# One attention-plus-MLP kernel: batch 0 mixed in transposed form in PSUM with its mask added by TensorE, and Q/K of batches 2 to 7 loaded twice as token pairs

## Chip, cores and metric

The kernel runs on one core of one Trainium2 chip. The metric is the device time of one execution in microseconds (us), the median of several runs. Here the time of a run is 1.8 us above the span (first to last instruction) that its profile shows. Each run is marked fast or slow in the record, because some executions of a kernel come out slower than the rest. The profile of before is of one further run (356.0 us), whose state the record calls unknown.

Engines: PE is TensorE (matmuls), PEld its weight loads, DVE VectorE, ACT ScalarE, POOL GpSimd, SP the queue that stores the output. "The queue" below is the one whose DMAs POOL issues; all loads of inputs that are cast from fp32 to bf16 go through it. PSUM is the memory into which the matmuls write. The granted clock is the share of PE's full clock that the profile shows as granted to it.

## The reference

Sliding-window attention (window 64, causal) on 8 batches of 8 heads, 576 tokens, head size 64, followed by a token-mixing low-rank step and an MLP:

```python
scores = (q @ k.T) / 8;  mask: 0 <= pos_q - pos_k < 64;  x = softmax(scores) @ v      # per head
h = x.T @ U @ V          # U (576, 32), V (32, 576): mixes tokens
u = x + h.T
out = u + relu(u @ w_ch1) @ w_ch2                                                     # (512, 2048), (2048, 512)
```

Inputs and output are fp32; the kernel computes matmuls in bf16.

## The kernel before

The 4608 tokens are cut into nine chunks of 512. The MLP of a chunk is 16 `ch1` pieces (four matmuls into `psA`, a ReLU on ACT or DVE) and 16 `ch2` pieces (four matmuls into `psU`). Attention of batch b + 1 is woven into the MLP of chunk b: every step of it is put behind a numbered piece, its slot. Batch 0 has no MLP to hide in; it is the prologue.

```python
RUN = [18, 18, 6, 2, 1, 2, 1, 6]        # consecutive tokens in one run of a K/Q load, by batch
PAIRED = [True] * 5 + [False] * 3       # True: 32-bit transpose, score matmuls of 32 rows, twice as many
                                        # False: loaded twice, 16-bit transpose, score matmuls of 64 rows
# ... (cut)
def KT(x, n):                           # transpose of raw K or Q on DVE
    ...
    nc.vector.transpose(                # the form for PAIRED False
        out=dst[:, n * S : (n + 1) * S].rearrange("q (m p e) -> q m e p", p=32, e=r), ...)
def SC(n):                              # scores of a tile on PE, exp on ACT, mask by multiplying on DVE
def PV(t):                              # 16 matmuls with V, 1/sum and product on DVE -> x
def UM(ts):  ...                        # hh = U.T x;  VM: un = x + V.T hh;  UT: transpose un on PE, copy to uT
# ... (cut)
load_v(0, both=True)                    # V of batch 0 comes twice, the second time shifted by 64 tokens (vB)
# ... (cut)
DVE_RELU = (1, 3, 5, 7, 9, 11, 13)      # ch1 pieces whose ReLU is on DVE; the others are on ACT
PLACE = {"VC": [0], "S": [1, 1, 4, 4, 7, 7], "PV": [10, 10, 13, 13, 15],
         "KT": [8, 9, 11, 12, 14, 16, 18, 19],              # KT of the batch after
         "U": [17], "V": [19, 20, 21], "UT": [21, 22, 23, 24, 25]}
PLACE_1 = {"KT": [6, 7, 8, 9], "S": [10, 10, 13, 13, 16, 16], "VC": [18],
           "PV": [20, 20, 22, 22, 24], "U": [26], "V": [28, 29, 30], "UT": [29, 30, 31, 31, 32]}
turn_over(24)                           # matmuls on zeros that keep PE busy; more between the steps of batch 0
```

`VC` copies V into its shifted form `vB` for the later batches (`pair_v`).

The softmax here doesn't subtract the row's maximum and nothing guards it: scores larger than these inputs give would overflow.

## Time and profile before

| | before |
|---|---|
| median time of three runs | 354.2 us (353.8 to 354.7) |
| PE busy | 327.1 us, 92% of the span of 354.1 |
| first `psA` matmul (end of prologue) | 32.2 |
| chunk 0 | 41.0 us |
| chunks 1, 2, 3, 4 | 35.6, 35.7, 35.5, 35.5 us |
| chunk 5 | 45.3 us |
| chunk 6, then 7 (no attention) | 34.1, 27.6 us |

A chunk's length is the time from its first `psA` matmul to the next chunk's first, read from the timeline of PE. This one table tells more than the shares of busy time: PE is the bound in every chunk, so a chunk is long where PE waits or its clock is low.

From the page of before: the span in 40 slices of 8.85 us, busy tenths, the granted PE clock in tenths of full speed, and the busy share of the DMA engines.

```profile
span 354.1 us, 7252 instructions
...
PE   8868997989999999999999999947899999999995
...
PEclk9958998999999999999999999999899999999999
DMA  7999999999999699959991911000010011011011
```

Counted from 1, the dips of PE are slices 1 to 4 (prologue), 7 and 9 (chunk 0) and 27 to 29 (chunk 5); in slices 3, 4, 7 and 29 the clock is down with it. The DMA row is full for the first 13 slices, 115 us.

The prologue, as a table of stretches (start:end, its length, busy time of PE, PEld, DVE, ACT and POOL with the number of instructions, granted clock, DMA share, GB/s):

```profile
8.60:15.60 7.00, 6.96 (x176) 3.68 (x176) 5.71 (x10) 4.45 (x6) 3.76 (x5) 1.00 2.90 155
15.60:25.20 9.60, 5.58 (x87) 3.17 (x87) 4.50 (x11) 1.43 (x4) 7.29 (x11) 0.63 3.07 135
25.20:32.20 7.00, 5.51 (x32) 2.23 (x32) 3.18 (x6) 2.93 (x5) 1.81 (x3) 0.77 1.16 212
```

From 15.6 to 25.2 PE works 5.6 of 9.6 us at a clock of 0.63: PV waits for the second copy of V. Two of PE's waits there, from the timeline (in brackets the idle time before, and what ended it; for a third, of 1.5 us to 19.0, the profile names nothing that ended it):

```profile
17.27 0.22 PE L322 MATMUL xr<-vB,pts 128*64 128x65 bf16 x1 [0.90 <-DMA vB<-in_v_dram]
...
22.92 0.23 PE L322 MATMUL xr<-vB,pts 128*64 128x65 bf16 x1 [1.29 <-DMA vB<-in_v_dram]
```

Chunk 5, from the chain of waits (start, us, what):

```profile
225.98 2.10 DVE kt L241
...
228.60 2.00 DVE qt L241
...
232.79 2.00 DVE kt L241
234.80 1.91 DVE qt L241
...
238.82 2.09 DVE kt L241
241.57 2.09 DVE qt L241
...
246.11 1.97 DVE qt L241
```

Batch 7's transposes, with runs of 6 tokens, take about 2 us each on DVE, and they are the chain: the ReLUs and PV products of chunk 5 stand behind them. With runs of 2, batch 5's transposes of the same form took 0.76 to 0.82 us.

### The profile page before, as it was taken

What the parts mean: (1) busy time and instruction counts of PE and PEld (TensorE: products, weight loads), DVE (VectorE), ACT (ScalarE), POOL (GpSimd) and SP (SyncE); (2) the same over time, 40 slices, a digit from 0 to 9 for tenths busy, and PEclk for the clock granted to TensorE, in tenths of its full rate; (3) what the DMA queues carried; (4) which work ended last, traced back from release to release, by engine and by line L of the source; (5) the groups of instructions that cost most, each with busy time, mean ns of one, the idle gap of its engine ahead of it and who ended that gap; (6) DMA issues with size and microseconds to landing.
All of it is one profiled execution on the core that took longest, in us unless ns stands there. A gap on an engine that the chain in (4) does not pass through costs nothing.

```text
span 354.1 us, 7252 instructions
## 1 busy us (share of the span) xinstructions
PE 327.1 (92%) x3046; PEld 155.6 (44%) x3046; DVE 207.1 (58%) x343; ACT 110.9 (31%) x177; POOL 137.3 (39%) x213
## 2 busy tenths in 40 slices
PE   8868997989999999999999999947899999999995
PEld 3433443445454445544444444422445454444442
DVE  5743846679654864578558855899456543313311
ACT  1604450155224523352235233510225232401300
POOL 8572328899999379927961300000000000000000
PEclk9958998999999999999999999999899999999999
DMA  7999999999999699959991911000010011011011
GB/s 127 141 154 212 206 165 135 175 146 128 111 178 172 61 83 168 171 37 97 174 181 11 58 61 61 2 0 31 30 61 2 0 61 59 0 61 59 0 48 74
DMA packets 101553, 32.78 MB, mean 93 GB/s; under 512 B 87568, under 2 KB 95248, under 8 KB 101520
## 3 DMA queue, kind: packets, MB, share of 16 engines
q0 software_dynamic: 94928, 22.43, 77.7%
q1 hardware_dynamic: 6592, 9.88, 8.1%
q8 instruction: 24, 0.39, 0.5%
q14 instruction: 9, 0.07, 0.1%
HBM read 45.27 MB, written 9.44 MB: 154 GB/s over the span
## 4 chain that ended last, share of the span: by engine, by line
PE 63%; DVE 14%; DMA 13%; issue 4%; POOL 3%; ACT 1%; DVEq 0%; POOLq 0%
PE psU L458 33%; PE psA L436 22%; DMA vA<-in_v_dram 8%; DMA w1b<-in_moe_w_ch_dram 3%; DVE qt L241 3%; DVE kt L241 2%; DVE c L445 2%; PE sc L288 2%; PE tpu L406 2%; DVE xs L332 2%; PE psv L371 2%; PE xr L322 2%; DMA qr<-in_q_dram 1%; DVE un L387 1%; ACT pts L296 1%
## 5 line engine op out<-in xcount | busy, mean ns | idle before, releaser
L458 PE MATMUL psU<-w2b,c 128*128 128x512 bf16 x576 | 137.3, 384 | 0.0
L436 PE MATMUL psA<-uTc,w1b 128*128 128x512 bf16 x576 | 131.3, 380 | 1.1 <-ACT uTc L411 0.7
L447 ACT ACTIVATE c<-psA 128x512 bf16<-128x512 f32 x81 | 48.5, 598 | 112.0 <-PE psA L436 112.0
L458 PEld LDWEIGHTS <-c 128*128 128x128 bf16 x576 | 54.3, 99 | 62.7 <-issue 6.5
L436 PEld LDWEIGHTS <-w1b 128*128 128x128 bf16 x576 | 53.8, 98 | 63.1 <-issue 1.3
L467 DVE TENSOR_TENSOR osb<-psU,un 128x512 f32<-128x512 f32 x36 | 25.0, 694 | 80.2 <-PE psU L458 80.2
L445 DVE TENSOR_SCALAR c<-psA 128x512 bf16<-128x512 f32 x63 | 42.9, 686 | 21.5 <-PE psA L436 21.3
L125 POOL DMA_DIRECT2D kr<-in_k_dram x76 | 47.6, 627 | 11.1 <-DMA w2b<-in_moe_w_ch_dram 4.2
L125 POOL DMA_DIRECT2D qr<-in_q_dram x76 | 47.0, 619 | 8.8 <-DVE pts L303 4.5
L131 POOL DMA_DIRECT2D vA<-in_v_dram x32 | 28.4, 894 | 37.5 <-PE xr L322 24.7
L296 ACT ACTIVATE pts<-sc 128x768 bf16<-128x768 f32 x48 | 36.6, 809 | 17.3 <-PE sc L288 15.7
L303 DVE TENSOR_TENSOR pts<-pts,mask 128x768 bf16<-128x768 bf16 x48 | 26.4, 556 | 18.9 <-ACT pts L296 15.7
L411 ACT COPY uTc<-tpu 128x512 bf16<-128x512 bf16 x32 | 18.8, 586 | 46.8 <-PE tpu L406 46.8
L322 PE MATMUL xr<-vB,pts 128*64 128x65 bf16 x320 | 16.9, 202 | 12.5 <-DVE xs L332 5.8
L332 DVE TENSOR_TENSOR xs<-xr,rcp 128x512 bf16<-128x512 f32 (+1 forms) x40 | 27.6, 691 | 1.4
L387 DVE TENSOR_TENSOR un<-psv,xs 128x512 bf16<-128x512 f32 (+1 forms) x38 | 24.3, 685 | 5.9 <-PE psv L371 5.7
L322 PEld LDWEIGHTS <-pts 128*64 128x64 bf16 x576 | 13.6, 115 | 25.9 <-DVE xs L332 14.3
L288 PEld LDWEIGHTS <-kt 32*64 32x64 bf16 (+1 forms) x1040 | 14.3, 105 | 11.8 <-issue 11.8
L288 PE MATMUL sc<-qt,kt 32*64 32x128 bf16 (+5 forms) x1040 | 17.5, 215 | 0.4 <-DVE qt L235 0.4
L406 PEld LDWEIGHTS <-un 128*128 128x128 bf16 x144 | 11.2, 100 | 13.0 <-issue 6.5
L508 PE MATMUL unread<-idle 128*128 128x512 bf16 (+1 forms) x52 | 15.3, 427 | 1.3 <-DVE idle L155 1.3
L371 PE MATMUL psv<-hh,vrep 128*128 128x512 bf16 x40 | 13.2, 392 | 3.5 <-DVE un L387 3.0
(51 smaller groups left out, 143.1 us busy)
## 6 DMA issues: line engine op xcount, KB each, us to landing
out_dram<-osb SPq DMA_DIRECT2D x36, 256.0 KB, 2.3
kr<-in_k_dram POOLq DMA_DIRECT2D x72, 72.0 KB, 4.1
qr<-in_q_dram POOLq DMA_DIRECT2D x72, 72.0 KB, 3.9
vA<-in_v_dram POOLq DMA_DIRECT2D x32, 128.0 KB, 4.7
w2b<-in_moe_w_ch_dram POOLq DMA_DIRECT2D x2, 1024.0 KB, 21.4
kr<-in_k_dram POOLq DMA_DIRECT2D x4, 288.0 KB, 9.4
qr<-in_q_dram POOLq DMA_DIRECT2D x4, 288.0 KB, 10.2
vB<-in_v_dram POOLq DMA_DIRECT2D x16, 64.0 KB, 6.8
```

Source lines behind the costliest of these rows:

```text
L125: nc.gpsimd.dma_start(out=o, in_=i)
L131: nc.gpsimd.dma_start(out=va[:, t, :, 0:D], in_=v[b, :, t * P : (t + 1) * P, :].rearrange("h p d -> p h d"),)
L288: nc.tensor.matmul(sc[half * W : (half + 1) * W, g, (a - lo) * W : (z - lo) * W], operand("k", g, jj, e, kb * W, (kb + 1) * W), operand("q ...
L296: nc.scalar.activation(out=dst, in_=sc[:, :, 0 : PB * W].rearrange("p g (n w) -> p g n w", w=W), func=ACT.Exp, scale=scale,)
L303: nc.vector.tensor_tensor(out=dst, in0=dst, in1=mask[:, m0 : m0 + PB, :].unsqueeze(1).to_broadcast([P, 2, PB, W]), op=ALU.mult,)
L322: nc.tensor.matmul(xr[r0 : r0 + W, h // 4, (h % 4) * VW : (h % 4 + 1) * VW], pts[:, g, jj * NB + blk, :], rhs, start=True, stop=True,)
L332: nc.vector.tensor_tensor(out=x[lo:hi, t, :, :].rearrange("p (a h) d -> p a h d", a=2), in0=xv[:, :, :, 0:D], in1=rcp[lo:hi].to_broadcast( ...
L387: nc.vector.tensor_tensor(out=u_tiles[g][rs, :], in0=ps[rs, n, :], in1=xt[n][rs], op=ALU.add)
L436: nc.tensor.matmul(ps[:], w1b[:, dc, i * P : (i + 1) * P], uTc[:, dc, :], start=(dc == 0), stop=(dc == NDC - 1),)
L445: nc.vector.tensor_relu(out=c1[i][:], in_=ps[:])
L447: nc.scalar.activation(out=c1[i][:], in_=ps[:], func=ACT.Relu)
L458: nc.tensor.matmul(acc[t][:], c1[i][:, t * P : (t + 1) * P], w2b[:, i, :], start=(i == 0), stop=(i == NFC - 1),)
```

## The change

Two main things at once, and the ReLU split, the places and the load order that go with them.

1. Q and K of batches 2 to 7 are all loaded twice with runs of two tokens (`PAIRED` False), with 8 larger DMAs per batch instead of 16 or 32. That removes the slow transposes of chunk 5 and gives batches 2 to 4 the 64-row score matmuls, at twice the bytes for those three batches.
2. Batch 0: V is loaded once; the mask is added as a bias of -1e30 by an identity matmul; u of batch 0 is mixed in transposed form. x is transposed into four banks of PSUM, the four `UP` matmuls add the mixing term there, and four copies give uT. That takes the place of V, UT and their serial copies.
3. ReLUs on DVE go from seven to five per chunk. Batches 1, 2 and 3 get later places, the first half of `w2` is now loaded before batch 1's K/Q, and the K/Q loads of batches 3 and 4 are issued from later slots (23 and 13, before 10 and 4). Batch 0's V is shifted into `vB` by copies, for two of its tiles on DVE and for two on POOL.

The core of the diff (long; cut at "..."):

```diff
-    RUN = [18, 18, 6, 2, 1, 2, 1, 6]
-    PAIRED = [True] * 5 + [False] * 3
+    RUN = [RP, RP] + [2] * (B - 2)
+    PAIRED = [True, True] + [False] * (B - 2)
...
+        def SC0(n):                       # batch 0: bias by TensorE, no mask multiply
...
+                    nc.tensor.matmul(sc[:, g, 0 : PB * W], ident[:], bias[...], start=True, stop=False)
...
+        def XT(t):                        # x transposed into PSUM
+            def f():
+                for dc in range(NDC):
+                    nc.tensor.matmul(xT0[:, dc, t * P : (t + 1) * P], x[:, t, 2 * dc : 2 * dc + 2, :]..., ident[:],
+                                     start=(t == 0), stop=False)
...
+        def UP():
+            for dc in range(NDC):
+                nc.tensor.matmul(xT0[:, dc, :], hh["sb"][:, dc * P : (dc + 1) * P], vrep[:, W : W + CH],
+                                 start=False, stop=True)
+            for dc in range(NDC):
+                copy = dve_copy if dc % 2 else nc.scalar.copy
+                copy(out=uT_of(0)[:, dc, :], in_=xT0[:, dc, :])
...
-    DVE_RELU = (1, 3, 5, 7, 9, 11, 13)
+    DVE_RELU = (1, 4, 7, 10, 13)
...
     PLACE_1 = {
-        "KT": [6, 7, 8, 9],
-        "S": [10, 10, 13, 13, 16, 16],
-        "VC": [18],
-        "PV": [20, 20, 22, 22, 24],
-        "U": [26],
-        "V": [28, 29, 30],
-        "UT": [29, 30, 31, 31, 32],
+        "KT": [16, 17, 19, 20],
+        "S": [19, 19, 21, 21, 23, 23],
+        "VC": [24],
+        "PV": [25, 25, 27, 27, 28],
+        "U": [29],
+        "V": [30, 31, 31],
+        "UT": [31, 31, 32, 32, 32],
     }
...
+    KT_3 = [17, 18, 20, 22, 24, 26, 28, 30]          # batch 3's transposes, in chunk 1
...
+    xT0 = psum["x0"].tile([P, NDC, CH], FP32, name="xT0")
...
-    turn_over(24)
+    turn_over(26)
...
-        turn_over(6 if n == 1 else 2)
+        turn_over(8 if n == 1 else 2)
...
+    load_w2(0, 8)
+    load_kq(1)
+    load_w2(8, 16)
+    load_v(1)
```

## The prediction

> **What bounds it now.** TensorE: the page gives PE 92% busy, and the chain of waits is 63% PE. An MLP chunk without attention takes 27.6 us (first psA to first psA, 294.96 to 322.59 in the chain); nine make 249 us. A chunk with a batch's attention takes at best 34.1 us (260.8 to 295.0, no wait of PE), usually 35.5. Three stretches are worse (chain, timeline):
> - 0 to 32.2 us, prologue. Scores end at 15.1; then PV waits for the second copy of V (vB DMAs; PV tiles start at 15.6, 17.3, 20.4, 22.9, 24.1), with a granted clock of 0.63 (windows, 15.6:25.2). U, V and UT run serially from 25.2.
> - Chunk 0, 32.2 to 73.3, 41.1 us: PV of batch 1 waits 3.1 us for vB, whose input lands only near 54; clock 0.84 in 52:62.5; a serial UT tail.
> - Chunk 5, 215.6 to 260.8, 45.3 us. Eight transposes of batch 7 with runs of 6 take 2.0 to 2.2 us each on DVE, against 0.73 to 0.82 with runs of 2 (batch 5, same form). PE waits there 3.4 + 2.7 + 1.0 us and more behind DVE, and the clock falls to 0.91.
>
> **What changes.**
> 1. Runs of 2 for batches 2 to 7. Chunk 5: 8 x 1.3 = 10 us less DVE, so it becomes an ordinary chunk: -10 us. Batches 2 to 4 go from 208 32-row score matmuls (1.94 us, chain) to 104 64-row ones (1.38): -0.55 us each. They pay 8 transposes (6.2 us) for 4 (3.0), but two ReLUs per chunk leave DVE (-1.4 us). Net -0.3 us per chunk.
> 2. Prologue: V loads once (0.6 MB, about 5 us of queue at the 135 GB/s seen); vB copies are about 0.2 us on DVE (64x2080 took 0.69). The mask multiply (0.56 us) leaves DVE for two bias matmuls per tile, about 0.35 us of PE. U, V, UT (7 us) become hh, four matmuls and four PSUM copies (about 3.5 us). PV should end near 20, first psA at 24 to 25: -7.5 us. Batch 0's adds move into chunk 0: +1.3 us of PE there.
> 3. Chunk 0: 27.6 + batch 1 (about 9 us PE) + 1.3 + a later-placed, serial UT tail (3 us) and small waits: about 42.5, no shorter than before. So the prologue's gain survives to about 67 us, minus 1.
>
> DMA: batches 2 to 4 load 2.36 MB instead of 1.18. POOL issues fall from 16 or 32 per batch at 0.6 us to 8 at about 0.95 (1024-descriptor V issues cost 0.88). Batch 6 moved twice as many packets in 21 us of issuing, so I estimate 13 to 17 us per batch, within a 35 us chunk.
>
> **Sum.** 67 + 35.3 + 4 x 35.1 + 34.1 + 27.6 + 27.6 + 4 = 336. Nearly all of it is on PE's path: about -10 chunk 5, -6.5 prologue and chunk 0, -1.5 elsewhere.
>
> The Trainium skill, "TensorE: Matmul & The Clock Gate", Part 1, says idle windows of about 3.4 us halve the clock; the 0.63 and 0.84 above agree. Fewer waits should give about 1.0 from 16 us on.
>
> **Right or wrong shows in**: first psA at 24 to 26; second chunk's at 66 to 69; no transpose above 0.9 us after batch 1; chunk 5 near 35; score bursts of 0.46.
>
> **What would spoil it**: the queue, now carrying twice the bytes for batches 2 to 4, lands K/Q of batch 3 or 4 after its transpose's place, so DVE stalls in order and PE with it (up to 8 us); POOL's copies of V delay the weight issues; a cold clock in the prologue; the bunched end of chunk 0.
>
> Chances: faster 0.95, within 2% 0.04, slower 0.01. Range 331 to 343.

## The result, and the profile after

The median went from 354.4 us (before, run again in these rounds) to 342.6 us. The ratio is 0.966, with an interval of 0.960 to 0.972: 3.4% faster. (A ratio here is the mean time of one kernel's fast runs over the mean of the other's in the same rounds, so not quite the ratio of the two medians.) The time lies in the predicted range, but the forecast gain was 18 us and the measured one 12.

The chunks of all versions, from the timeline of PE (us; the second column is where the prologue ends, the fourth is where chunk 1 starts; prologue and chunk 0 together):

| version | first psA | chunk 0 | chunk 1 starts | 1 | 2 | 3 | 4 | 5 | median |
|---|---|---|---|---|---|---|---|---|---|
| before | 32.2 | 41.0 | 73.2 | 35.6 | 35.7 | 35.5 | 35.5 | 45.3 | 354.4 |
| my prediction | 24.5 | 42.5 | 67 | 35.3 | 35.1 | 35.1 | 35.1 | 35.1 | 336 |
| after | 28.5 | 46.2 | 74.7 | 35.7 | 35.0 | 34.2 | 35.0 | 34.2 | 342.6 |
| pairs_alone | 31.6 | 42.7 | 74.3 | 41.8 | 35.6 | 34.8 | 35.6 | 34.8 | 350.6 |
| pairs_late | 33.0 | 41.2 | 74.2 | 34.3 | 35.6 | 34.8 | 35.6 | 34.8 | 344.2 |
| batch0_alone | 28.3 | 45.1 | 73.4 | 36.4 | 35.1 | 34.9 | 34.9 | 44.6 | 352.0 |
| relu_7 | 27.6 | 45.9 | 73.5 | 35.2 | 35.6 | 34.8 | 35.6 | 34.8 | 344.7 |
| four_tiles | 26.4 | 43.7 | 70.0 | 35.7 | 35.0 | 34.2 | 35.0 | 34.2 | 339.1 |
| few_fillers | 27.2 | 45.7 | 72.9 | 35.4 | 35.0 | 34.2 | 35.0 | 34.2 | 341.6 |
| chunk0_early | 27.8 | 39.9 | 67.7 | 34.3 | 35.0 | 34.2 | 35.0 | 34.2 | 336.3 |
| early_four | 26.7 | 44.0 | 70.7 | 34.2 | 35.0 | 34.2 | 35.0 | 34.2 | 338.8 |
| all_three | 25.4 | 45.9 | 71.3 | 34.3 | 35.0 | 34.2 | 35.0 | 34.2 | 339.0 |
| v1_first | 27.1 | 38.6 | 65.7 | 40.2 | 35.0 | 34.2 | 35.0 | 34.2 | 339.3 |
| v1_first_few | 23.9 | 40.9 | 64.8 | 39.0 | 35.0 | 34.2 | 35.0 | 34.2 | 337.7 |
| kt3_later | 26.9 | 38.6 | 65.6 | 33.9 | 35.0 | 34.2 | 35.0 | 34.2 | 332.3 |

The row of after says it: chunks 1 to 5 together give 13 us (11 of them chunk 5), and the prologue with chunk 0 gives nothing. It ends 1.5 us later than before.

The same rows of the page as of before (slices of 8.55 us):

```profile
span 342.2 us, 6690 instructions
...
PE   8996996969999999999999999999999999999995
...
PEclk9998999889999999999999999999999999999998
DMA  7999999999999999995999291000100010011011
```

PE is near full from slice 10 on, and chunk 5 is no longer to be seen: the transposes of batches 2 to 7 now take 0.76 to 0.82 us each. From the page (count | busy us, mean ns of one | idle before):

```profile
L242 DVE STREAM_TRANSPOSE kt<-kr 128x576 bf16<-128x576 bf16 x24 | 19.3, 804 | 0.0
```

What is left are dips of PE in slices 1, 4, 7 and 9, with a clock of 0.8 in 4, 8 and 9. The DMA row is full for 18 slices now, 154 us.

The stretches of the prologue and chunk 0 after:

```profile
9.10:18.50 9.40, 9.40 (x191) 4.64 (x189) 3.15 (x7) 4.45 (x6) 6.78 (x12) 1.00 1.65 117
18.50:23.00 4.50, 4.50 (x104) 3.41 (x103) 3.79 (x10) 0.41 (x1) 4.50 (x8) 1.00 1.22 191
...
26.00:40.00 14.00, 11.49 (x46) 4.96 (x47) 6.63 (x10) 4.46 (x8) 3.84 (x5) 0.88 1.17 207
...
48.00:58.00 10.00, 8.51 (x188) 4.30 (x185) 4.88 (x8) 4.54 (x6) 7.64 (x10) 1.00 1.71 161
58.00:66.00 8.00, 6.80 (x87) 3.46 (x88) 7.35 (x15) 0.00 (x0) 3.29 (x5) 0.79 2.51 166
66.00:74.70 8.70, 5.81 (x41) 2.75 (x39) 4.24 (x7) 2.93 (x5) 3.43 (x5) 0.97 1.90 202
```

The wait for V is gone (18.5 to 23: PE full, clock 1.00). But the scores now take until 18.5 where they ended near 15.6, and four stretches later PE loses 1.2 to 2.9 us each, with a clock of 0.88 and 0.79 in two of them.

The score stage, by its exp (ACT; in brackets its idle time before), first in before, then in after:

```profile
13.17 0.81 ACT L296 ACTIVATE pts<-sc 128x768 bf16<-128x768 f32 x1 [0.21 <-PE sc L288]
14.19 0.81 ACT L296 ACTIVATE pts<-sc 128x768 bf16<-128x768 f32 x1 [0.21 <-PE sc L288]
...
15.42 0.81 ACT L303 ACTIVATE pts<-sc 128x768 bf16<-128x768 f32 x1 [0.52 <-PE sc L295]
16.75 0.81 ACT L303 ACTIVATE pts<-sc 128x768 bf16<-128x768 f32 x1 [0.53 <-PE sc L295]
```

A tile took 1.02 us and now takes 1.33; the exp is as long as before and waits longer for PE.

The end of the prologue, in the timeline (start, us, engine, line, operation, in brackets the idle time before it and what ended it):

```profile
25.71 0.58 ACT L482 CAST uTc<-xT 128x512 bf16<-128x512 f32 x1 [1.13 <-PE xT L473]
26.33 0.69 DVE L482 CAST uTc<-xT 128x512 bf16<-128x512 f32 x1 [2.80 <-ACT uTc L482]
27.05 0.58 ACT L482 CAST uTc<-xT 128x512 bf16<-128x512 f32 x1 [0.76 <-DVE uTc L482]
27.67 0.69 DVE L482 CAST uTc<-xT 128x512 bf16<-128x512 f32 x1 [0.65 <-ACT uTc L482]
...
28.51 0.81 PE L503 MATMUL psA<-uTc,w1b 128*128 128x512 bf16 x3 [2.83 <-DVE uTc L482]
```

Four copies of 0.58 to 0.69 us on two engines run one after another, each released by the one before; PE stands 2.8 us.

### The profile page after: what moved, and what is told of

Same layout as the page of the kernel before. It is cut to its first block, busy times and chain, and to the rows that moved or that the text cites. A ratio compares the mean times of both kernels' runs of the same rounds, so it can differ in the third digit from the quotient of the medians.

```text
span 342.2 us, 6690 instructions
## 1 busy us (share of the span) xinstructions
PE 327.1 (96%) x2830; PEld 153.6 (45%) x2830; DVE 195.3 (57%) x339; ACT 119.5 (35%) x190; POOL 90.1 (26%) x121
## 4 chain that ended last, share of the span: by engine, by line
PE 70%; DMA 11%; DVE 10%; POOL 4%; issue 2%; ACT 1%; DVEq 0%; POOLq 0%
PE psU L525 31%; PE psA L503 29%; DMA w2b<-in_moe_w_ch_dram 7%; PE xr L371 2%; DVE un L427 2%; PE sc L337 2%; PE tpu L442 2%; DMA kr<-in_k_dram 2%; DMA vA<-in_v_dram 2%; DVE qt L242 2%; DVE xs L381 2%; DVE osb L534 1%; PE psv L416 1%; PE pshh L397 1%; DVE kt L242 1%
## 5 line engine op out<-in xcount | busy, mean ns | idle before, releaser
L514 ACT ACTIVATE c<-psA 128x512 bf16<-128x512 f32 x99 | 59.3, 599 | 99.1 <-PE psA L503 98.5
L512 DVE TENSOR_SCALAR c<-psA 128x512 bf16<-128x512 f32 x45 | 30.7, 683 | 40.7 <-PE psA L503 40.6
L124 POOL DMA_DIRECT2D vA<-in_v_dram x32 | 28.2, 885 | 65.7 <-PE xr L371 43.8
L345 ACT ACTIVATE pts<-sc 128x768 bf16<-128x768 f32 x42 | 31.7, 808 | 14.5 <-PE sc L337 11.8
L446 ACT COPY uTc<-tpu 128x512 bf16<-128x512 bf16 x32 | 18.7, 585 | 41.8 <-PE tpu L442 41.8
L381 DVE TENSOR_TENSOR xs<-xr,rcp 128x512 bf16<-128x512 f32 (+1 forms) x40 | 27.6, 691 | 1.4
L112 POOL DMA_DIRECT2D kr<-in_k_dram x24 | 19.9, 829 | 25.4 <-DVE kt L242 12.3
L112 POOL DMA_DIRECT2D qr<-in_q_dram x24 | 20.1, 837 | 8.9 <-DVE qt L242 4.6
L242 DVE STREAM_TRANSPOSE kt<-kr 128x576 bf16<-128x576 bf16 x24 | 19.3, 804 | 0.0
L242 DVE STREAM_TRANSPOSE qt<-qr 128x576 bf16<-128x576 bf16 x24 | 19.0, 792 | 0.0
L371 PE MATMUL xr<-vB,pts 128*64 128x65 bf16 x320 | 15.9, 198 | 1.8 <-DVE vB L136 1.1
L406 ACT CAST hh<-pshh 128x512 bf16<-128x512 f32 x8 | 4.7, 585 | 35.6 <-PE pshh L397 35.6
L580 PE MATMUL xT<-idle 128*128 128x512 bf16 (+2 forms) x62 | 15.9, 389 | 1.3 <-DVE idle L140 1.3
L442 PE MATMUL tpu<-ident,un 128*128 128x128 bf16 x128 | 12.5, 221 | 2.7 <-ACT uTc L446 2.0
```

The source lines that it names most:

```text
L112: nc.gpsimd.dma_start(out=dst[32 * part : 32 * (part + 1), off : off + NJJ * RD].rearrange("p (n x) -> p n x", x=r * D), in_=src[b, m * NJ ...
L124: nc.gpsimd.dma_start(out=va[:, t, :, 0:D], in_=v[b, :, t * P : (t + 1) * P, :].rearrange("h p d -> p h d"),)
L242: nc.vector.transpose(out=dst[:, n * S : (n + 1) * S].rearrange("q (m p e) -> q m e p", p=32, e=r), in_=src[:, 32 + n * RD : 32 + (n + 1) ...
L345: nc.scalar.activation(out=dst, in_=sc[:, :, 0 : PB * W].rearrange("p g (n w) -> p g n w", w=W), func=ACT.Exp, scale=scale,)
L371: nc.tensor.matmul(xr[r0 : r0 + W, h // 4, (h % 4) * VW : (h % 4 + 1) * VW], pts[:, g, jj * NB + blk, :], rhs, start=True, stop=True,)
L381: nc.vector.tensor_tensor(out=x[lo:hi, t, :, :].rearrange("p (a h) d -> p a h d", a=2), in0=xv[:, :, :, 0:D], in1=rcp[lo:hi].to_broadcast( ...
```

## The experiments

Twelve kernels ran, all correct.

### Which of the two parts brings the gain

**pairs_alone**: before, with the K/Q loads of the change only.

```diff
-    RUN = [18, 18, 6, 2, 1, 2, 1, 6]
-    PAIRED = [True] * 5 + [False] * 3
+    RUN = [RP, RP] + [2] * (B - 2)
+    PAIRED = [True, True] + [False] * (B - 2)
     # and load_kq, the raw tiles and the transposes' slices as in after
```

> The kernel before with only the K/Q loading of the change (token pairs, twice, batches 2 to 7; order and places as before). Theory 1, the pair loads carry the whole gain and the batch 0 rewrite nothing: 341 to 343 us, chunk 5 (batch 6's attention, batch 7's transposes) 35.3 us as chunk 4 was before, chunk 0 41 us and first psA at 32.2 unchanged. Rival, the rewrite is worth several us and the pair loads less: 346 or more. A third way, the doubled loads land late for before's earlier places (batch 2's transposes at the start of chunk 1): chunk 1 or 2 above 38 us.

Measured: 350.6 us, ratio 0.987 (0.981 to 0.992). Chunk 5 falls to 34.8 us as the theory had it, but chunk 1 rises to 41.8: the third way came true. (The total alone would also have fitted the rival, "346 or more"; the chunks decide.) The timeline of DVE in chunk 1 (the first two transposes of batch 3):

```profile
90.24 0.81 DVE L240 STREAM_TRANSPOSE kt<-kr 128x576 bf16<-128x576 bf16 x1 [4.06 <-issue]
...
92.77 0.81 DVE L240 STREAM_TRANSPOSE qt<-qr 128x576 bf16<-128x576 bf16 x1 [1.17 <-DMA vA<-in_v_dram]
```

DVE stands 4.1 and 1.2 us in front of them, in the middle of the ReLUs, because batch 3's doubled K/Q has not landed. (The label of the first wait is "issue"; the second names a DMA. The last of batch 3's K/Q was issued at 79.0, with a median of 12 us to landing in this stretch.)

**pairs_late**: pairs_alone with after's places for batches 2 and 3.

```diff
-    PLACE_2["KT"] = [0, 0, 1, 1, 2, 2, 3, 3]      # and the rest of batch 2, as in after
+    "KT": [5, 6, 7, 8, 9, 10, 11, 12],
+    KT_3 = [17, 18, 20, 22, 24, 26, 28, 30]
-                slots[4].append(lambda: load_kq(4))
+                slots[13].append(lambda: load_kq(4))
```

> pairs_alone with after's places for batches 2 and 3 (batch 2's KT in slots 5 to 12, batch 3's KT from slot 17, batch 4's load in slot 13). pairs_alone lost 41.8 us in chunk 1 against 35.6, where DVE stood 4.1 us in front of batch 3's first transpose. Theory: that is the doubled load of batch 3 landing after the early place, so the later places bring chunk 1 to 35.3 to 36.3 and the total to 344 to 346. Rival: the queue has no room for the doubled loads beside V loaded twice; then the wait moves on to batch 3's or 4's transposes in chunks 1 and 2, one of them stays above 38, total above 347.

Measured: 344.2 us, ratio 0.968 (0.964 to 0.971); chunk 1 is 34.3 us. The theory holds. The later places are part of what makes the doubled loads pay.

**batch0_alone**: after, with before's K/Q loads.

```diff
-    RUN = [RP, RP] + [2] * (B - 2)
-    PAIRED = [True, True] + [False] * (B - 2)
+    RUN = [18, 18, 6, 2, 1, 2, 1, 6]
+    PAIRED = [True] * 5 + [False] * 3
     # and load_kq, the raw tiles and the transposes' slices as in before
```

> The kernel after with before's K/Q loading (runs 18,18,6,2,1,2,1,6, five batches paired); all else as after. Theory 1: chunk 5 is back at about 45 us, first psA at 28.5, second chunk's at about 74.5; total 353 to 355 us, no faster than before. Rival (the doubled pair loads crowd the queue in chunk 0 and cost it 3 to 4 us): second chunk's first psA at 70 to 71, total 349 to 351.

Measured: 352.0 us, ratio 0.992 (0.986 to 0.998). Chunk 5 is back at 44.6 us. Chunk 1 starts at 73.4, as in before (73.2). Its total is 1 us under the expected band; the next run accounts for that. The rival, that the doubled loads cost chunk 0 three to four us, falls: taking them away moves chunk 1's start by 1.3 us, no more than one profile differs from another there (relu_7, below, has after's chunk 0 and 73.5).

**relu_7**: after, with before's split of ReLUs.

```diff
-    DVE_RELU = (1, 4, 7, 10, 13)
+    DVE_RELU = (1, 3, 5, 7, 9, 11, 13)
```

> The kernel after with before's seven DVE ReLUs per chunk instead of five. pairs_late had 35.6 and 34.8 in chunks 2 to 5 where after has 35.0 and 34.2. Theory: the ReLU split alone is that difference: relu_7 has 35.6 and 34.8 there, total 2.2 to 3 us above after, 344.8 to 345.8. Rival: the difference comes from batch 0's rewrite or the queue; relu_7 keeps 35.0 and 34.2 and 342 to 343.

Measured: 344.7 us against 342.6 of after, so 2.1 us, just under the expected step; chunks 2 to 5 are 35.6 and 34.8, each 0.6 us longer, as expected. So the ReLU split is worth about 2 us: 0.6 us in each of four chunks, 2.1 by the medians, 1.5 by the ratios (0.970 and 0.966, whose intervals overlap). With it the books close: pairs_late (344.2) less 2.1 is 342.1, and after is 342.6, within the noise of a per cent or less. The rewrite of batch 0, with the places and the load order that it came with, brought nothing that can be seen.

### Why the prologue and chunk 0 gained nothing

**four_tiles**: after, with the tile `xT0` of four banks as four tiles of one bank.

```diff
-    xT0 = psum["x0"].tile([P, NDC, CH], FP32, name="xT0")
+    xT0 = [psum["x0"].tile([P, CH], FP32, name=f"xT0_{i}") for i in range(NDC)]
     # uses: xT0[:, dc, ...] -> xT0[dc][:, ...]
```

> The kernel after with the four-bank PSUM tile of batch 0 split into four one-bank tiles, so that the four copies to uT no longer wait for one another. Theory: the copies ran one after another (25.7 to 28.4 us) only because of the shared tile: now two engines work side by side, first psA at about 27.2 instead of 28.5, and the clock dips less; 341 to 342 us. Rival: the copies' time is hidden or moves on to chunk 0's waits for batch 1, whose K/Q and V arrival sets chunk 0's end: first psA earlier, second chunk's first psA still at 74.7, total unchanged within 0.3 us.

Measured: 339.1 us, ratio 0.954 (0.949 to 0.959), 3.5 us faster than after and better than expected. The copies overlap:

```profile
24.74 1.07 ACT L482 CAST uTc<-xT 128x512 bf16<-128x512 f32 x2 [0.48 <-PE xT L473]
24.96 1.29 DVE L482 CAST uTc<-xT 128x512 bf16<-128x512 f32 x2 [1.75 <-PE xT L473]
...
26.39 1.02 PE L503 MATMUL psA<-uTc,w1b 128*128 128x512 bf16 x4 [1.04 <-DVE uTc L482]
```

In the built program of after each copy waits for the other engine's copy before it; with four tiles each waits only for its matmul. The order came from the shared tile, not from the chip. PE's wait falls from 2.8 to 1.0 us, and from the first `hh` matmul to the first `psA` it is now 3.6 us where after took 5.4. First psA comes 2.1 us earlier in this pair of profiles. (Over all profiles, versions with the one tile and all fillers ended the prologue at 27.6 to 28.5, those with four tiles at 26.4 to 27.1, so 1.3 to 1.8 us is the safer figure.) Chunk 0 shrinks by 2.5 us too, and the clock is at least part of the reason:

```profile
26.40:40.00 13.60, 13.55 (x63) 6.17 (x65) 6.08 (x10) 5.38 (x9) 3.85 (x5) 1.00 1.17 206
```

After had 0.88 from 26 to 40, by estimate 0.12 x 14 = 1.7 us. The second slow stretch, 0.79 from 58 to 66 in after, is gone as well (1.00 from 55 to 70); why is not shown. The Trainium skill, "TensorE: Matmul & The Clock Gate", Part 1, says that an idle window of about 3.4 us halves the clock, that full speed comes back only after a busy window, and that matmuls of 512 columns start 427 ns apart while it is halved. The trace of after agrees on the half and on the spacing: the granted clock is 0.50 from 29.75 to 33.16, and from 29.84 to 32.83 its weight loads start every 0.43 us. On the length of the idle window it does not settle the matter (last section).

```profile
30.27 0.15 PEld L503 LDWEIGHTS <-w1b 128*128 128x128 bf16 x1 [0.28 <-issue]
30.70 0.15 PEld L503 LDWEIGHTS <-w1b 128*128 128x128 bf16 x1 [0.28 <-issue]
```

**few_fillers**: after, with fewer matmuls on zeros.

```diff
-    turn_over(26)
+    turn_over(23)
-        turn_over(8 if n == 1 else 2)
+        turn_over(2 if n == 1 else 0)
```

> The kernel after with 23 instead of 26 filler matmuls before batch 0's scores, and in the score stage 2 in place of 18. Theory: PE, not exp, sets the score stage's step in after (1.33 us: bias 0.43, scores 0.46, fillers 0.43), the fillers are a real cost there: scores end at about 15.5 to 16 instead of 18.5, PV is then held by the copies of V on POOL (done at 18.9), first psA at 26 to 27 instead of 28.5, total 340 to 341.5. Rival: without fillers the clock falls below 0.8 in 9:23 and eats it: first psA at 28 or later, total 342 or more.

Measured: 341.6 us, ratio 0.960 (0.955 to 0.965). First psA at 27.2, within 0.2 us of the expected band; the total is 0.1 us above its band. The total is not clear of noise against after (0.960 to 0.972). Both theories have a part: without the fillers the scores do end at 15.6, and the clock falls to 0.72 from 18.5 to 23. Of the 18.5 - 15.6 = 2.9 us at most 1.3 came back, and less if the spread of the prologue's end from profile to profile is counted. The clock is 0.50 from 17.6 to 21.0, after a wait of PE of 1.05 us in PV's second tile (15.9 to 17.0) for which the profile names no cause. The next bound that the expectation named, POOL's copies of V, does not show: they end from 17.0 to 19.0, and the PV tiles that read them start at 17.9, 19.4 and 20.8, each later than its own copy.

**chunk0_early**: after, with batch 1's K/Q ahead of `w2` and batch 1 at before's places.

```diff
-    load_w2(0, 8)
     load_kq(1)
+    load_w2(0, 8)
     load_w2(8, 16)
-        "KT": [16, 17, 19, 20],                   # PLACE_1, all of it as in before
+        "KT": [6, 7, 8, 9],
```

> The kernel after with batch 1's K/Q loaded ahead of w2, and batch 1's attention in chunk 0 at before's places (KT 6 to 9, scores 10 to 16, PV 20 to 24). Theory 2, the late bunched places cost chunk 0 its fill (scores to uT run 48.6 to 74.7 with 8 MLP pieces left to hide PV, U, V, UT): chunk 0 falls from 46.2 to 41.5 to 43 us, total 338.5 to 340. Rival, the arrival of weights and V over the full queue sets chunk 0's end whatever the places: chunk 0 stays above 45.5, total 342 or more (w2 half a megabyte later could even cost).

Measured: 336.3 us, ratio 0.949 (0.942 to 0.957), 6.3 us faster than after and better than expected. Chunk 0 falls to 39.9 us, and chunk 1 to 34.3. So the late, bunched places, together with the load order, were the largest single loss: in after batch 1's scores start at 48.6 and its PV near 60 with six pieces of MLP left, and PE runs dry between the DVE and ACT steps. The end of chunk 0 in after (to 74.7), then here (to 67.7):

```profile
58.00:74.70 16.70, 12.61 (x127) 6.21 (x127) 11.59 (x21) 2.93 (x5) 6.72 (x10) 0.88 2.19 185
...
58.00:67.70 9.70, 8.30 (x55) 4.02 (x54) 6.27 (x10) 2.93 (x5) 4.01 (x5) 1.00 1.97 206
```

Chunk 1's 1.4 us fit the clock: in after it is 0.50 from 74.1 to 77.5, the start of chunk 1; here it is 1.00 there. Two things were changed, and no run parts them, but the traces allow an estimate. In after batch 1's K/Q are issued from 20.5 to 22.1 and take 15.7 to 18.2 us to land, so they are there from 36.2 to 40.3. Here the four transposes that read them start at 36.1, 38.3, 39.4 and 40.5. After's load order would hardly have held these places up, so by this estimate nearly all of the gain is the places'.

### What bounds chunk 0 then

**early_four**: four_tiles and chunk0_early together.

> four_tiles and chunk0_early together. If the two are independent: second chunk's first psA at 67.7 - 2 = about 65.7, total 333 to 334.5. If V of batch 1 (landing near 50.4 in chunk0_early) sets chunk 0's end: first psA at 26.4, but second chunk's still at 67 to 67.7, total 335.5 to 336.5.

Measured: 338.8 us, ratio 0.953 (0.950 to 0.956). It is no faster than chunk0_early alone, although its prologue ends 1.1 us earlier. (By the medians it is 2.5 us slower; the intervals of the two ratios overlap.) In its profile chunk 1 starts at 70.7, 3.0 us later than there and worse than both expectations. The longest waits of PE in 20 to 70 (line, tile, releaser: us in total, times, longest), then of DVE in 25 to 70:

```profile
PE xr L371 <- DVE vB L136: 4.0, 1, 4.0
```

```profile
DVE vB L136 <- DMA vA<-in_v_dram: 4.9, 1, 4.9
```

DVE waits 4.9 us for V of batch 1, which lands near 51.8, and PE 4.0 us behind it. The clock pays again: 0.79 from 50 to 58. In chunk0_early, which reached the same place a little later, V landed near 50.4, DVE waited 0.8 us, and the clock stayed at 1.00 from 50 to 58. The same line there:

```profile
DVE vB L136 <- DMA vA<-in_v_dram: 0.8, 1, 0.8
```

So an earlier start became a wait, and the wait became a cold clock. Why V landed 1.4 us later here was not settled.

**all_three**: with few_fillers as well.

> four_tiles, chunk0_early and few_fillers together. First psA at 24 to 25 (the prediction's value). If independent: second chunk's first psA at 63.5 to 65, total 331 to 333. If V of batch 1 sets chunk 0's end: chunk 0 stretches to 42 or more, second chunk at 66.5 to 67.7, total 335 to 336.5, no better than early_four.

Measured: 339.0 us, ratio 0.954 (0.952 to 0.956). First psA at 25.4, not at 24 to 25; DVE waits 7.0 us for V (landing near 52.7), PE 6.1, and the clock is 0.57 from 50 to 58. Chunk 1 starts at 71.3. "V of batch 1 sets chunk 0's end" holds, "independent" falls. The total is 2.5 us above the band; neither expectation had that V would land 2.3 us later than in chunk0_early, nor the half clock (0.50 from 50.5 to 57.3, of which PE works from 53.5 on: about 1.9 us by estimate).

**v1_first**: early_four, with V of batch 1 ahead of the second half of `w2`.

```diff
     load_w2(0, 8)
-    load_w2(8, 16)
     load_v(1)
+    load_w2(8, 16)
```

> early_four with V of batch 1 loaded ahead of w2's second half. In early_four PE stood 4.0 us in chunk 0 in front of PV because V of batch 1 landed near 52, last in the queue, and the clock fell to 0.79. Theory: it is the order of arrival. V then lands about 5 us earlier (1.05 MB at the 205 GB/s seen), the wait and the clock dip go, w2's second half is needed 4 pieces later and is just in time: second chunk's first psA at 66 to 67.5, total 334 to 336. Rival: the queue as a whole is full until about 52 us, so the wait only moves to w2's second half: second chunk's first psA at 69.5 or later, total 337.5 or more.

Measured: 339.3 us, ratio 0.953 (0.949 to 0.957). Chunk 0 is mended as the theory had it (38.6 us, chunk 1 starts at 65.7, PE waits 0.7 us for `w2`), yet the total is that of early_four, because chunk 1 takes 40.2 us. Timeline of DVE in chunk 1, batch 3's first two transposes, then PE's longest wait in 64 to 107:

```profile
86.95 0.82 DVE L242 STREAM_TRANSPOSE kt<-kr 128x576 bf16<-128x576 bf16 x1 [2.85 <-DMA vA<-in_v_dram]
89.18 0.82 DVE L242 STREAM_TRANSPOSE qt<-qr 128x576 bf16<-128x576 bf16 x1 [1.41 <-DMA vA<-in_v_dram]
```

```profile
PE xr L371 <- DVE xs L381: 4.6, 2, 4.2
```

It is pairs_alone's wait once more: chunk 1 came 2 us earlier than in chunk0_early, batch 3's doubled K/Q did not. The half clock follows here too (0.50 from 92.0 to 95.4).

**v1_first_few**: v1_first with few_fillers' score stage.

> v1_first with few_fillers' shorter score stage (first psA at 25.4 instead of 26.7 in these versions). Theory, the queue's end near 52 is the floor of chunk 0: 1.3 us earlier start gives nothing or at most 0.5 us, total within 0.7 us of v1_first. Rival, the start counts in full once V is early: 1.3 us faster than v1_first.

Measured: 337.7 us, two of six runs slow; ratio 0.945 (0.939 to 0.950) against v1_first's 0.953 in the same rounds, which is 0.9% or about 3 us. The prologue ends at 23.9, but of its lead of 3.2 us only 0.9 is left where chunk 1 starts; in chunk 0 PE now waits 1.8 us for `w2`, where v1_first waited 0.7, and chunk 1 still waits (39.0 us). Neither theory gave this size, its fast runs spread from 333.8 to 338.1, and the two left out as slow (338.9 and 339.3) lie just above them, so I take nothing from it but the pattern.

**kt3_later**: v1_first, with batch 3's transposes placed later in chunk 1.

```diff
-    KT_3 = [17, 18, 20, 22, 24, 26, 28, 30]
+    KT_3 = [22, 23, 24, 25, 27, 28, 30, 31]
```

> v1_first with batch 3's transposes in chunk 1 from slot 22 instead of 17. v1_first gained in chunk 0 (second chunk's first psA at 65.7) and lost it in chunk 1 (40.2 us against 34.25), where DVE stood 2.9 + 1.4 us in front of batch 3's transposes and PE 4.2 us behind DVE. Theory: batch 3's K/Q lands near 89 to 90 because the queue has been full since the start, and only transposes placed before that cost anything: chunk 1 falls to 34.3 to 35.5, total 333 to 335, the fastest version. Rival: the doubled load of batch 4 behind it now comes late for chunk 2: chunk 1 is mended, chunk 2 goes above 38, total 336 or more.

Measured: 332.3 us, ratio 0.936 (0.932 to 0.939), 0.7 us under the expected band. Chunk 1 is 33.9 us and chunk 2 stays at 35.0, so the rival falls. PE's waits in 20 to 145:

```profile
PE tpu L442 <- ACT uTc L446: 1.3, 2, 0.7
PE psA L503 <- DVE uTc L482: 1.0, 1, 1.0
PE psU L525 <- DMA w2b<-in_moe_w_ch_dram: 0.8, 1, 0.8
```

Nothing above 1.3 us is left in this window, and the clock is 1.00 throughout 26 to 100. This is the fastest version: 6.5% under before, and, by the two ratios to before, 0.9355 / 0.9657 = 0.969, about 3% under after.

## Why the prediction was right or wrong

The range held the time and the direction was right. Of its own signs two came true (no transpose above 0.9 us after batch 1: 0.82; chunk 5 near 35: 34.2) and two failed (first psA 28.5 for 24 to 26; the second chunk's 74.7 for 66 to 69). The centre was 6 us low, and two errors of opposite sign are in it, which in part hid each other: that chunks 2 to 5 came out 2.0 us better than forecast was not foreseen. The sum is also one of a span, and the 1.8 us between span and run time were left out of it. Against the profiled span of 342.2 (of the slowest of the four runs, 344.0) the sum reads: chunk 1's start 74.7 for 67 (+7.7), chunk 1 35.7 for 35.3 (+0.4), chunks 2 to 5 138.4 for 140.4 (-2.0), the rest +0.1.

- **Chunk 5: right.** "-10 us" was -11.1. batch0_alone brings the 44.6 us back, pairs_alone takes them away. It is nearly the whole gain of the change.
- **Chunks 2 to 4: right in sign, too small.** "Net -0.3 us per chunk" was -0.7, -1.3 and -0.5. I had set the ReLUs' relief off against more transposes on DVE; relu_7 shows the ReLU split alone to be 0.6 us per chunk of PE time.
- **Prologue: mis-sized.** "-7.5 us" was -3.7 (to -4.6 in the other profiles with this prologue). The term "hh, four matmuls and four PSUM copies (about 3.5 us)" measured 5.4: it fits copies that run as two pairs side by side; they ran in a row, and four_tiles, with 3.6 us for this term, returns 1.3 to 2.1 us. The rest is the score stage: I counted 0.35 us of PE for the bias but not that PE, with its fillers, would thus take over from the exp as the pace of that stage (1.33 us a tile where it had been 1.02). few_fillers returns up to 1.3 us of that. With both mended, all_three and v1_first_few end the prologue at 25.4 and 23.9, about where the prediction had it. "vB copies are about 0.2 us on DVE": they took 0.27 to 0.29 us there, and half of them went to POOL, at 0.61 to 0.63.
- **Chunk 0: this step failed.** "So the prologue's gain survives to about 67 us" was wrong; nothing survived. I had chunk 0 at 42.5 and it was 46.2. I named "the bunched end of chunk 0" and "a cold clock in the prologue" among the spoilers and then put small numbers on them. chunk0_early shows the places, with the load order, to be worth 6.3 us; in four_tiles, with a wait of PE shortened from 2.8 to 1.0 us, the time at half clock after it is gone.
- **The queue: named as a risk, not treated as a bound.** In after itself it costs little (PE's longest wait for `vB` in chunk 0 is 1.1 us), since the later places go around it. It costs as soon as one stops going around it: 6 us in chunk 1 of pairs_alone, 4.0 us of PE in early_four, 4.2 us in v1_first. In v1_first K/Q and V of batch 2 and K/Q of batch 3, 2.36 + 0.59 + 2.36 = 5.3 MB, came in between about 51.5, where `w2` was done, and 89: 140 GB/s, or 17 us for a doubled batch, the upper end of my "13 to 17 us". The rate was right, but I had not added up arrivals: everything up to batch 3's K/Q stands in one line from the start, and that line ends near 90 us.
- **Clock "about 1.0 from 16 us on": half right.** It is 1.00 from 18.5 to 26, then 0.88 (26 to 40) and 0.79 (58 to 66), and 0.50 from 74.1 to 77.5. The two low stretches of before that the prediction names, 0.63 and 0.84, came with waits of PE of at most 1.5 and 2.6 us (1.7 and 3.1 between weight loads), so they bear out the low clock after waits but not an idle window of 3.4 us.

What is not settled: how much of before's choice to place batch 1 early would have paid in after without the reordered load (the two were changed together in chunk0_early; the estimate there says nearly all, no run does), and why V's landing moved from 50.4 to 51.8 and 52.7 between versions that issue it within 1.5 us. (In all_three part of it comes from further up: the first `w1` load was issued 1.7 us later than in early_four, at 16.4 for 14.7.)

## What to carry to other kernels

A gain at the start of a kernel is worth only what the next shared resource lets through: add up when each load lands, in the order of the queue, and compare that with the earliest time at which each step could now run, before counting a saved microsecond. When a load gets larger, move the steps that read it, because a step that waits on an in-order engine stops everything placed behind it there. And a matrix engine that waits can pay twice, once for the wait and once for a low clock after it: here that followed waits of 2.2 us (pairs_late) and 2.8 us (after), though not one of 3.4 us (before). So a version that starts earlier can end no earlier, as early_four did.

## What the Trainium skill lacked or had wrong

- "TensorE: Matmul & The Clock Gate", "Back-to-back issue gap", gives about 131 ns per matmul as the measured sustained spacing at 512 columns. Here 64 such matmuls, each with its weight load, take 13.81 us: 216 ns, the page's own figure for an isolated gap.
- The same page, Part 1, ties the slow clock to an idle window of about 3.4 us, and calls the window free-running. Here the length of a wait did not decide, and shorter ones were enough. A wait of PE of 2.8 us (25.7 to 28.5 in after; 3.3 us between weight loads) was followed by matmuls 0.43 us apart, and one of 2.2 us (53.8 to 56.0 in pairs_late) by a clock of 0.50 from 57.2 to 60.6. One of 1.0 us (four_tiles) was not, and neither was one of 3.4 us (234.7 to 238.1 in before), after which the clock stayed at 1.00 until 250.3. (A free-running window may explain the last, as no window need lie inside the wait; it does not explain how 2.2 and 2.8 us were enough. First the wait, then the stretch after it.)

```profile
238.11 0.45 PE L322 MATMUL xr<-vB,pts 128*64 128x65 bf16 x8 [3.38 <-DVE xs L332]
...
236.62:240.03 3.41, 1.92 (x16) 1.03 (x16) 3.34 (x7) 0.00 (x0) 0.00 (x0) 1.00 0.02 5
```

- "GPSIMD Engine Reference", "Engine selection", calls one-input elementwise work on GpSimd roughly line-rate, and about 2x slower only for two inputs. Here the same one-input bf16 copy, 64x520, took 0.61 to 0.63 us on POOL and 0.27 to 0.29 us on DVE, so about twice as long too.
- None of the pages that I read says that two engines' copies out of different banks of one PSUM tile may be ordered one behind the other by the program built around them: 2.7 us for four copies here, against 1.5 us with one tile per bank.
- "DMA: Bandwidth & Descriptors", "Anatomy of one DMA", says that many descriptors can be emitted before the incremental cost shows, and puts no figure on that generation. Here an issue of K/Q took POOL 0.62 us on average in before (nearly all of 72 KB) and 0.83 us in after (288 KB): the statement agrees, and eight large issues cost POOL far less than 32 small ones.
